# Half copies and a new product order in joined gate/up blocks, with sums between HBM tensors in longer rows

## Chip, core and metric

One core of one Trainium2 chip. The metric is the device time of the kernel in microseconds, the median of the runs of one comparison. Engines are named as in the profile: PE (TensorE, matmuls), PEld (its weight loads), DVE (VectorE), ACT (ScalarE), POOL (GpSimd), SP (the queue that issues the loads).

## What is computed

With S = 2048 rows, D = 512 and F = 1792, all in float32:

```python
g = sigmoid((x * gate_w).sum(-1))            # one gate per row
a = x @ dft_hid_re.T ; b = x @ dft_hid_im.T  # DFT over the 512 columns
A = dft_seq_re @ a - dft_seq_im @ b          # DFT over the 2048 rows, real part
B = (relu(x @ W_gate) * (x @ W_up)) @ W_down # gated ReLU unit
out = g * A + (1 - g) * B
```

## The kernel before

**Arithmetic.** Each operand is split into a high and a low part in fp32r, and a product is three matmuls (lo by hi, hi by lo, hi by hi; `PARTS`). Products of 2x2 block matrices are done by the seven-product scheme of Strassen and Winograd, `LEFT` and `RIGHT` being the sums that go into products 1 to 7. A product over one 512-column half is 6 matmuls of 128x128 by 128x512. There are 3423 matmuls.

**PSUM.** Its eight banks form four pairs x, m, y, t (`PAIRS`), one bank for each half i of a product. `BANK` says where a product accumulates: 1 and 2 in x, 5 and 3 in m, 6 and 7 in y, 4 in t. Product 1 is copied from x to y, and 6 and 7 go on accumulating there; the value of y after product 6 (`s6`) and that of m after product 5 (`s5`) are copied to SBUF. After product 7 ACT copies -y to t, on which product 4 accumulates, and DVE adds u22 = y + s5. After product 3 DVE adds u12 = m + s6.

**Stages in order.** The gate/up stage has 7 block columns c: two at the start (for q=0 alone), c=2 by `Block` for q=0 and q=1, then c=3 to 6, in each of which one `Joined` block for q=0 and one for q=1 share a product set with `JointW` (the left-out corner products of both q, 3 matmuls each, in bank pair x; their evacuations are jv and jo). `JointX` makes the x forms (jx) for them once. In `Joined` the q=0 block has product 1 in y rather than x. Then come four spectral blocks (the DFT over columns: spectral for q=0 twice, q=1 twice), two late gate/up blocks (`Block(1, ...)`), two Down stages, and the Sequence, Joint and Last stages (the DFT over rows). In the profile the c=2 blocks end at 82 us, the spectral blocks begin at 233, the late blocks take 311 to 349.

**Other streams around these.** Results of a gate/up block (h0, h1 and their sums hs) are stored to the HBM tensor hd by POOL. POOL also issues `joint_sums` (l.1052): 32 DMAs from HBM to HBM, half of them accumulating, that form sums of the DFT matrices in the tensor td, which the Joint stages read from 528 us on. Gates (`gate`) load x rows (gx) on SP, reduce on DVE and put sigmoids in gs; `gate_store` writes them to HBM. `h_late` reloads h of a block (hk) and makes the sums that were left out at the start. The matrix x21 of q=1 is loaded and split again ahead of the spectral stage, since its buffers were given up.

**What sets the order.** The program records steps with a key, the index of a matmul: `pe(n, ...)` adds n matmuls, `op(key, ...)` any other step. `Plan.due` works back from the matmuls when a step must be done, and `Plan.order` goes through all engines and picks steps by a table of costs written in the kernel. The steps are emitted in that order, so each engine runs its own list in order, and 51 SBUF buffers of 4 KB a partition are handed from step to step, the longest idle first. DMAs on SP and POOL are issued in order as well, each behind those ahead of it. Every instruction is recorded by line 126. Two engines that read one PSUM bank are put one behind the other.

Of the kernel before, what the change touches and what calls it, by code (L numbers as in the profile page):

```python
# [10 lines left out]
AF = mybir.ActivationFunctionType  # L11
# [4 lines left out]
N = 512  # L16
# [112 lines left out]
class Plan:  # L129
# [14 lines left out]
    def op(self, key, f, *a):  # L144
        self.ops.append((key, len(self.ops), f, a))

    def pe(self, n, f, *a):
        self.op(self.now, f, *a)
        self.now += n
# [129 lines left out]
def kernel(ctx: ExitStack, tc, xP, xG, wgu, wd, cr, ci, wri, gw, out):  # L279
# [24 lines left out]
    plan = Plan()  # L304
    op, pe = plan.op, plan.pe
# [7 lines left out]
    td = hbm("td", 2, 4, 2, P, 2, N)  # L313
# [31 lines left out]
    def E():  # L345
        return plan
# [4 lines left out]
    def f32(ap):  # L351
        return ap.bitcast(F32)

    def combine(o, a, b, sign):
        (plan.vector.tensor_add if sign > 0 else plan.vector.tensor_sub)(o, a, b)
# [4 lines left out]
    def store(o, i, **k):  # L360
        plan.gpsimd.dma_start(out=o, in_=i, **k)

    def accumulate(o, i, **k):
        plan.gpsimd.dma_start(out=o, in_=i, accum_op=OP.add, **k)
# [9 lines left out]
    def x_load(q, b, ks=slice(0, 2)):  # L374
        k, j, o = int(b[0]) - 1, int(b[1]) - 1, piece[q, b]
        return lambda: load(o[:, ks], xP[2 * q + j, k, :, ks])
# [132 lines left out]
    class Block:  # L509
# [31 lines left out]
        def evac(self, m, key):  # L541
            x, y, p, t = (self.banks[k] for k in "xymt")
            e = E()

            def rectified(r, j, ps, sign):
                g, h = self.g[r], self.h[int(r[0]) - 1][:, j]
                op(key, lambda: e.scalar.activation(g.all, ps[0], AF.Relu, scale=sign))
                if sign > 0:
                    op(key + 1, lambda: e.vector.tensor_mul(h, g.all, ps[1]))
                else:  # L550
                    op(key + 1, lambda: e.vector.scalar_tensor_tensor(h, ps[1], sign, g.all, op0=OP.mult, op1=OP.mult))

            def added(r, ps, s):
                self.added(r, ps, s, key)

            if m == 1:
                op(key, lambda: e.scalar.copy(y.all, x.all))
            elif m in (5, 6):
                op(key, lambda: e.scalar.copy(self.s[m].all, (p if m == 5 else y).all))
            elif m == 2:  # L560
                rectified("11", 0, x, 1.0)
            elif m == 7:
                op(key, lambda: e.scalar.activation(t.all, y.all, AF.Copy, scale=-1.0))
                added("22", y, self.s[5])
            elif m == 3:
                added("12", p, self.s[6])
            elif m == 4:
                rectified("21", 0, t, -1.0)
# [7 lines left out]
    class Joined(Block):  # L576
# [6 lines left out]
                self.s[1] = buf("s1")  # L583

        def run(self, joint=None):
            slots = {(1, 1): (5, 1), (6, 1): (6,), (3, 0): (3, 7), (3, 1): (2, 4)}
            for m, i in (*((m, i) for m in ((1, 5) if self.q else (5, 1)) for i in range(2)), (6, 0), (6, 1), (3, 0), (7, 0), (7, 1), (3, 1), (4, 0), (4, 1)):
                pe(6, self.product, m, i)
                if i:
                    self.evac(m, plan.now)  # L590
                for y in slots.get((m, i), ()) if joint else ():
                    joint.step(y)
# [5 lines left out]
        def one(self, m, i, k, n):  # L598
            w, x, ps = self.w.of(m, i, k), self.x[m], self.banks["y" if m == 1 and not self.q else BANK[m]]
            a, b = PARTS[n]  # L600
            mm(ps[i], w[a], x[b][:, k], start=m in FIRST and k == n == 0, stop=m in (3, 4) and k == 1 and n == 2)

        def evac(self, m, key):
            y, t = self.banks["y"], self.banks["t"]
            if m == 1 and not self.q:
                op(key, lambda: E().scalar.copy(self.s[1].all, y.all))
            elif m == 7:
                for i in range(2):
                    op(key, lambda i=i: E().scalar.activation(t[i], y[i], AF.Copy, scale=-1.0))
                self.added("22", y, self.s[5], key)  # L610
            else:
                super().evac(m, key)

    class JointX:


        def __init__(self, key):
            a, b = (piece[q, "21"] for q in range(2))
            raw = [buf(f"jx{n}") for n in range(2)]
            t5, t6, t7, t4 = raw[0][:, 0], raw[0][:, 1], raw[1][:, 0], raw[1][:, 1]  # L620
            self.x = {}
            for n, (y, src, f) in enumerate((
                    (1, a[:, 0], None), (5, t5, (b[:, 0], a[:, 0])), (6, t6, (b[:, 1], t5)), (3, b[:, 1], None),
                    (7, t7, (b[:, 1], b[:, 0])), (2, a[:, 1], None), (4, t4, (a[:, 1], t6)))):
                x = self.x[y] = buf(f"jx{y}", dtype=F32R)
                if f:
                    op(key + 16 * n, lambda src=src, f=f: combine(src, *f, -1))
                op(key + 16 * n + 4, lambda x=x, src=src: E().scalar.copy(x[:, 0], src))
                op(key + 16 * n + 8, lambda x=x, src=src: E().vector.tensor_sub(x[:, 1], src, f32(x[:, 0])))

    class JointW:

# [419 lines left out]
    def joint_sums(m, hh, key):  # L1052
        def c(b):
            return (cr, ci)[m][2 * int(b[1]) - 2, 1, 2 * int(b[0]) - 2 + hh]

        for n, (o, first, second) in enumerate(((0, "11", "12"), (1, "12", "22"), (2, 0, "22"), (3, 2, "21"))):
            op(key + 30 * n, lambda o=o, i=first: store(td[m, o, hh], c(i) if isinstance(i, str) else td[m, i, hh], max_dma_last_dim=2 * N))
            op(key + 30 * n + 15, lambda o=o, i=second: accumulate(td[m, o, hh], c(i), max_dma_last_dim=2 * N))

# [77 lines left out]
    w = ws[1]  # L1139

    for n in range(4):
        joint_sums(n // 2, n % 2, 300 + 150 * n)

    spectral = Spectral()

# [5 lines left out]
    for c in range(2, NP):  # L1151
        w = prepared(c)
        if c == 2:
            for b in ("22", "11", "12", "21"):
                x_piece(1, b)
                op(plan.now - 100, x_load(1, b))
            for n, m in enumerate(ORDER):
                x_prep(1, m, plan.now - 46 + 24 * n)
            jx = JointX(plan.now + 70)
            for q in range(2):  # L1160
                Block(q, w).run()
        else:
            pair = [Joined(q, w) for q in range(2)]
            joint = JointW(w, jx, plan.now)
            for q, b in enumerate(pair):
                b.run(None if q else joint)
                b.done(plan.now + 8, joint)
    for q in range(2):
        x_piece(q, "21")
        op(plan.now - 150 + 60 * q, x_load(q, "21"))  # L1170
        x_prep(q, 2, plan.now - 100 + 100 * q)

    for t in range(NT):
        gate(t, plan.now + 30 + 50 * t)
    op(plan.now + 300, gate_store)
    for n, b in enumerate(BLOCKS):
        op(plan.now - 84 + n, spectral.load, b)
# [8 lines left out]
        return Left(source)  # L1186

    for c in range(2):
        h_late(0, c, plan.now + 30 * c)
    lefts = [spectrum(f) for f in range(2)]  # L1190
    for ih in range(2):
        SpectralBlock(spectral, 1, ih)
# [5 lines left out]
    key = plan.now  # L1198
# [83 lines left out]
```

## Time and profile before

| | us |
|---|---|
| median of the runs (788.25, 789.84, 790.48) | 789.84 |
| profiled execution | 789.34 |
| its span | 787.6 |
| PE busy | 779.2 |
| DVE busy | 635.0 |
| ACT busy | 403.6 |
| POOL busy | 116.4 |

The prediction quotes rows of four views. The page has busy times and the chain that ended last. The timeline has one instruction in a row: start in us, duration in us (a PE duration is a modelled end, so matmuls overlap; look at starts), engine, line, operation, output<-inputs by buffer name without number, shape, and in brackets the idle time of the engine just before it with what ended that. The view of a tile tells who waited for it. A group row has the count, busy us and mean ns of one.

### The profile page before, as it was taken

The numbers are of one execution on the slowest core, as the hardware profiler recorded it, in microseconds if no ns is written. First come the engines' busy times: TensorE is split into PE (matmuls) and PEld (weight loads), VectorE is DVE, ScalarE is ACT, GpSimd is POOL, SyncE is SP. The second block draws the span as 40 slices with busy tenths as digits, with TensorE's granted clock in tenths as the row PEclk, the third lists the DMA queues.
The fourth block names the chain that finished last, engine by engine and source line by source line (L and its number), as shares of the span: only waits on it lengthen the run. The fifth ranks groups of instructions, "written<-read, shape, count | busy, mean of one in ns | idle before, by whom it ended". The sixth has DMA issues, their size and how long they took to land.

```text
span 787.6 us, 9450 instructions
## 1 busy us (share of the span) xinstructions
PE 779.2 (99%) x3423; PEld 641.2 (81%) x3423; DVE 635.0 (81%) x700; ACT 403.6 (51%) x465; POOL 116.4 (15%) x160
## 2 busy tenths in 40 slices
PE   9999999999999999999999999999999999999997
PEld 7888788888887888888888888888888888888885
DVE  6999886868689423988764899977999999989963
ACT  6665443434355334476545464544757365565540
POOL 0020342333212121110000000200020001000200
PEclk9999999999999999999999999999999999999999
DMA  8373799979976998488688789849999889599914
GB/s 324 126 263 101 212 286 232 258 196 270 308 228 239 347 419 304 134 270 292 187 270 319 272 299 322 196 151 288 378 328 285 246 262 187 166 326 373 249 33 81
DMA packets 64287, 197.52 MB, mean 251 GB/s; under 512 B 6768, under 2 KB 15216, under 8 KB 64240
## 3 DMA queue, kind: packets, MB, share of 16 engines
q1 hardware_dynamic: 36656, 119.31, 42.5%
q0 software_dynamic: 27584, 77.60, 37.7%
q8 instruction: 27, 0.44, 0.2%
q14 instruction: 20, 0.16, 0.1%
HBM read 135.53 MB, written 69.75 MB: 261 GB/s over the span
## 4 chain that ended last, share of the span: by engine, by line
PE 84%; DMA 6%; issue 5%; DVE 2%; POOL 2%; ACT 1%; SPq 0%; POOLq 0%; ACTq 0%; DVEq 0%
PE ps L126 84%; DMA td<-ci 3%; DMA hd<-hs 2%; DMA td<-td 2%; POOL td L126 1%; POOL hd L126 1%; DVE u L126 1%; DVE h L126 1%; DMA wr<-wgu 0%; DVE hs L126 0%; ACT jch L126 0%; DVE v L126 0%; DVE z L126 0%; DVE vl L126 0%; DVE xl L126 0%
## 5 line engine op out<-in xcount | busy, mean ns | idle before, releaser
L126 PE MATMUL ps<-ch,ll 128*128 128x512 f32 x580 | 225.6, 389 | 0.0
L126 PE MATMUL ps<-cl,lh 128*128 128x512 f32 x580 | 225.6, 389 | 0.0
L126 PE MATMUL ps<-ch,lh 128*128 128x512 f32 x580 | 225.6, 389 | 0.0
L126 ACT CAST ch<-r 128x1024 fp32r<-128x1024 f32 x96 | 97.2, 1051 | 63.2 <-DVE r L126 52.6
L126 PEld LDWEIGHTS ps<-cl,lh 128*128 128x128 f32 x580 | 108.9, 188 | 22.7
L126 PEld LDWEIGHTS ps<-ch,ll 128*128 128x128 f32 x580 | 108.9, 188 | 22.6
L126 PEld LDWEIGHTS ps<-ch,lh 128*128 128x128 f32 x580 | 108.9, 188 | 22.5
L126 DVE TENSOR_TENSOR cl<-r,ch 128x1024 fp32r<-128x1024 f32 x96 | 114.6, 1219 | 2.4 <-ACT ch L126 2.0
L126 ACT COPY s<-ps 128x1024 f32<-128x1024 f32 x48 | 48.8, 1016 | 65.6 <-PE ps L126 59.4
L126 ACT ACTIVATE ps<-ps 128x1024 f32<-128x1024 f32 (+1 forms) x42 | 33.8, 805 | 89.0 <-PE ps L126 59.5
L126 DVE TENSOR_TENSOR cl<-hr,ch 128x1024 fp32r<-128x1024 f32 (+1 forms) x56 | 59.5, 1087 | 18.4 <-ACT ch L126 16.5
L126 ACT CAST ch<-hr 128x1024 fp32r<-128x1024 f32 (+1 forms) x56 | 51.4, 944 | 27.3 <-PE ps L126 19.7
L126 POOL DMA_DIRECT2D out<-z x23 | 17.0, 739 | 316.2 <-DVE z L126 310.9
L126 DVE TENSOR_TENSOR r<-r,r 128x1024 f32<-128x1024 f32 x48 | 57.1, 1218 | 0.0
L126 PE MATMUL ps<-xh,wb0l 128*128 128x512 f32 x112 | 44.0, 393 | 0.5 <-DVE u L126 0.5
L126 PE MATMUL ps<-vh,xl 128*128 128x512 f32 x112 | 43.7, 390 | 0.7 <-ACT s L126 0.7
L126 PE MATMUL ps<-xh,wb1l 128*128 128x512 f32 x112 | 43.9, 392 | 0.1
L126 PE MATMUL ps<-vl,xh 128*128 128x512 f32 x112 | 43.7, 390 | 0.0
L126 PE MATMUL ps<-xl,wb0h 128*128 128x512 f32 x112 | 43.6, 389 | 0.0
L126 PE MATMUL ps<-xh,wb0h 128*128 128x512 f32 x112 | 43.6, 389 | 0.0
L126 PE MATMUL ps<-vh,xh 128*128 128x512 f32 x112 | 43.6, 389 | 0.0
L126 PE MATMUL ps<-xl,wb1h 128*128 128x512 f32 x112 | 43.6, 389 | 0.0
(152 smaller groups left out, 1334.3 us busy)
## 6 DMA issues: line engine op xcount, KB each, us to landing
hr<-hd SPq DMA_DIRECT2D x42, 512.0 KB, 4.5
r<-cr SPq DMA_DIRECT2D x32, 512.0 KB, 6.8
r<-ci SPq DMA_DIRECT2D x32, 512.0 KB, 8.2
hd<-hs POOLq DMA_DIRECT2D x28, 512.0 KB, 8.8
out<-z POOLq DMA_DIRECT2D x23, 512.0 KB, 6.6
ad<-a POOLq DMA_DIRECT2D x16, 512.0 KB, 8.4
l<-ad SPq DMA_DIRECT2D x16, 512.0 KB, 8.0
r<-r POOLq DMA_DIRECT2D x16, 512.0 KB, 7.8
```

Of the source, the lines that this page charges most:

```text
L126: getattr(getattr(nc, self.engine), self.name)(*map(ap, self.a), **{k: ap(x) for k, x in self.k.items()})
```

## The change

1. **Order in joined blocks** (`Joined.run`). Before, q=0 began with products 5, 1 and q=1 with 1, 5; then 6, (3, half 0), (7, half 0), (7, half 1), (3, half 1), 4. Now both have 1, 5, 6, (3, 0), (7, 0), (3, 1), (7, 1), 4. The joint products 5 and 1 come behind (5, 1).
2. **Halves** (`half`). The copy to s6 behind product 6 and the copy of -y to t behind product 7 are issued for each half as soon as it is done. u22 is added behind both.
3. **JointX** starts at matmul +50 rather than +70, at a spacing of 12 rather than 16.
4. **joint_sums**: rows of 4 KB (8N bytes) instead of 1 KB; one set's steps are 50 matmuls apart rather than 15; sets begin at 300+130n rather than 300+150n.
5. **Later**: the load of x21 of q=1 from -90 to +70 (relative to the spectral start), and its split from 0 to +120; gates from +30+50t to +70+60t; the late sums from +30c to +180+40c.

The matmuls are the same in number and kind.

```diff
@@ -583,9 +583,11 @@
                 self.s[1] = buf("s1")
 
         def run(self, joint=None):
-            slots = {(1, 1): (5, 1), (6, 1): (6,), (3, 0): (3, 7), (3, 1): (2, 4)}
-            for m, i in (*((m, i) for m in ((1, 5) if self.q else (5, 1)) for i in range(2)), (6, 0), (6, 1), (3, 0), (7, 0), (7, 1), (3, 1), (4, 0), (4, 1)):
+            slots = {(5, 1): (5, 1), (6, 1): (6,), (3, 0): (3, 7), (3, 1): (2, 4)}
+            for m, i in [(m, i) for m in (1, 5, 6) for i in range(2)] + [(3, 0), (7, 0), (3, 1), (7, 1), (4, 0), (4, 1)]:
                 pe(6, self.product, m, i)
+                if m in (6, 7):
+                    self.half(m, i, plan.now)
                 if i:
                     self.evac(m, plan.now)
                 for y in slots.get((m, i), ()) if joint else ():
@@ -600,15 +602,20 @@
             a, b = PARTS[n]
             mm(ps[i], w[a], x[b][:, k], start=m in FIRST and k == n == 0, stop=m in (3, 4) and k == 1 and n == 2)
 
+        def half(self, m, i, key):
+            y = self.banks["y"][i]
+            if m == 6:
+                op(key, lambda: E().scalar.copy(self.s[6][:, i], y))
+            else:
+                op(key, lambda: E().scalar.activation(self.banks["t"][i], y, AF.Copy, scale=-1.0))
+
         def evac(self, m, key):
-            y, t = self.banks["y"], self.banks["t"]
+            y = self.banks["y"]
             if m == 1 and not self.q:
                 op(key, lambda: E().scalar.copy(self.s[1].all, y.all))
             elif m == 7:
-                for i in range(2):
-                    op(key, lambda i=i: E().scalar.activation(t[i], y[i], AF.Copy, scale=-1.0))
                 self.added("22", y, self.s[5], key)
-            else:
+            elif m != 6:
                 super().evac(m, key)
 
     class JointX:
@@ -624,9 +631,9 @@
                     (7, t7, (b[:, 1], b[:, 0])), (2, a[:, 1], None), (4, t4, (a[:, 1], t6)))):
                 x = self.x[y] = buf(f"jx{y}", dtype=F32R)
                 if f:
-                    op(key + 16 * n, lambda src=src, f=f: combine(src, *f, -1))
-                op(key + 16 * n + 4, lambda x=x, src=src: E().scalar.copy(x[:, 0], src))
-                op(key + 16 * n + 8, lambda x=x, src=src: E().vector.tensor_sub(x[:, 1], src, f32(x[:, 0])))
+                    op(key + 12 * n, lambda src=src, f=f: combine(src, *f, -1))
+                op(key + 12 * n + 4, lambda x=x, src=src: E().scalar.copy(x[:, 0], src))
+                op(key + 12 * n + 8, lambda x=x, src=src: E().vector.tensor_sub(x[:, 1], src, f32(x[:, 0])))
 
     class JointW:
 
@@ -1054,8 +1061,8 @@
             return (cr, ci)[m][2 * int(b[1]) - 2, 1, 2 * int(b[0]) - 2 + hh]
 
         for n, (o, first, second) in enumerate(((0, "11", "12"), (1, "12", "22"), (2, 0, "22"), (3, 2, "21"))):
-            op(key + 30 * n, lambda o=o, i=first: store(td[m, o, hh], c(i) if isinstance(i, str) else td[m, i, hh], max_dma_last_dim=2 * N))
-            op(key + 30 * n + 15, lambda o=o, i=second: accumulate(td[m, o, hh], c(i), max_dma_last_dim=2 * N))
+            op(key + 100 * n, lambda o=o, i=first: store(td[m, o, hh], c(i) if isinstance(i, str) else td[m, i, hh], max_dma_last_dim=8 * N))
+            op(key + 100 * n + 50, lambda o=o, i=second: accumulate(td[m, o, hh], c(i), max_dma_last_dim=8 * N))
 
 
 
@@ -1139,7 +1146,7 @@
     w = ws[1]
 
     for n in range(4):
-        joint_sums(n // 2, n % 2, 300 + 150 * n)
+        joint_sums(n // 2, n % 2, 300 + 130 * n)
 
     spectral = Spectral()
 
@@ -1156,7 +1163,7 @@
                 op(plan.now - 100, x_load(1, b))
             for n, m in enumerate(ORDER):
                 x_prep(1, m, plan.now - 46 + 24 * n)
-            jx = JointX(plan.now + 70)
+            jx = JointX(plan.now + 50)
             for q in range(2):
                 Block(q, w).run()
         else:
@@ -1167,11 +1174,11 @@
                 b.done(plan.now + 8, joint)
     for q in range(2):
         x_piece(q, "21")
-        op(plan.now - 150 + 60 * q, x_load(q, "21"))
-        x_prep(q, 2, plan.now - 100 + 100 * q)
+        op(plan.now - 150 + 220 * q, x_load(q, "21"))
+        x_prep(q, 2, plan.now - 100 + 220 * q)
 
     for t in range(NT):
-        gate(t, plan.now + 30 + 50 * t)
+        gate(t, plan.now + 70 + 60 * t)
     op(plan.now + 300, gate_store)
     for n, b in enumerate(BLOCKS):
         op(plan.now - 84 + n, spectral.load, b)
@@ -1186,7 +1193,7 @@
         return Left(source)
 
     for c in range(2):
-        h_late(0, c, plan.now + 30 * c)
+        h_late(0, c, plan.now + 180 + 40 * c)
     lefts = [spectrum(f) for f in range(2)]
     for ih in range(2):
         SpectralBlock(spectral, 1, ih)

```

**Where it moves instructions.** First DVE's list at the change from c=2 to c=3, from the last steps of the q=1 block of c=2. u22 and u12 are that block's sums, ps is PSUM, ws, wal, wb0l and wb1l are weights of c=3, jws and jw the joint weights, jx the joint x forms, h the results. Before:

```order
L126 TENSOR_TENSOR wb0l_700<-ws0_677,wb0h_694 128x1024
L126 TENSOR_TENSOR jws_707<-wr0_626 128x128
L126 TENSOR_TENSOR u22_711<-ps_76,s5_648 128x1024
L126 TENSOR_TENSOR jws_707<-jws_707,wr0_626 128x128
L126 TENSOR_TENSOR jws_707<-wr0_626 128x128
L126 TENSOR_TENSOR jws_707<-wr0_626,jws_707 128x128
L126 TENSOR_TENSOR h0_725<-g11_681,ps_76 128x512
L126 TENSOR_TENSOR ws1_732<-wr0_626,wr1_641 128x512
L126 TENSOR_TENSOR jw_728<-jws_707,jw_728 128x512
L126 TENSOR_TENSOR u12_744<-ps_76,s6_665 128x1024
L126 TENSOR_TENSOR ws1_732<-wr0_626,ws0_677 128x512
```
After:

```order
L126 TENSOR_TENSOR ws0_679<-ws0_679,wr0_631 128x512
L126 TENSOR_TENSOR jx7_684<-jx1_663,jx7_684 128x512
L126 TENSOR_TENSOR jws_712<-wr0_631 128x128
L126 TENSOR_TENSOR jws_712<-jws_712,wr0_631 128x128
L126 TENSOR_TENSOR u22_717<-ps_76,s5_650 128x1024
L126 TENSOR_TENSOR wb0l_725<-ws0_679,wb0h_708 128x1024
L126 TENSOR_TENSOR jws_712<-wr0_631 128x128
L126 TENSOR_TENSOR jws_712<-wr0_631,jws_712 128x128
L126 TENSOR_TENSOR h0_736<-g11_691,ps_76 128x512
L126 TENSOR_TENSOR jx4_698<-jx1_663,jx4_698 128x512
L126 TENSOR_TENSOR u12_747<-ps_76,s6_667 128x1024
L126 TENSOR_TENSOR jw_739<-jws_712,jw_739 128x512
```
u22 now stands ahead of wb0l and has no wait on ACT any more; ACT's copy of -y waits for it instead. u12 follows the x form jx4 and comes ahead of jw and ws1.

Then ACT's list in the q=1 block of c=5 from the copy of product 1 to the halves of -y: s5 and s6 are the copies out of PSUM, the two ACTIVATE rows of 512 columns copy -y to t by halves, CAST rows split weights. Before:

```order
L126 COPY ps_76<-ps_76 128x1024
L126 COPY s5_1527<-ps_76 128x1024
L126 CAST wah_1539<-wr0_1490 128x1024
L126 CAST jw_1551<-jws_1525 128x512
L126 COPY s6_1556<-ps_76 128x1024
L126 CAST wb0h_1563<-ws0_1546 128x1024
L126 ACTIVATE ps_76<-ps_76 128x512 x2
```
After:

```order
L126 COPY ps_76<-ps_76 128x1024
L126 COPY s5_1528<-ps_76 128x1024
L126 CAST wah_1539<-wr0_1493 128x1024
L126 COPY s6_1548<-ps_76 128x512
L126 CAST jw_1555<-jws_1534 128x512
L126 COPY s6_1548<-ps_76 128x512
L126 CAST wb0h_1571<-ws0_1560 128x1024
L126 ACTIVATE ps_76<-ps_76 128x512 x2
```
s6 was one row of 1024 columns behind the jw cast; it is two of 512 now, and the first stands ahead of that cast.

Last POOL's list in c=6 and at the spectral start, with the td sums from HBM to HBM and the stores of h to hd. Before:

```order
L126 DMA hd_68<-hs0_1647 128x2x512
L126 DMA hd_68<-hs1_1656 128x2x512
L126 DMA td_70<-td_70 512x256
L126 DMA td_70<-ci 512x256
L126 DMA hd_68<-h0_1764 128x512
L126 DMA hd_68<-h1_1741 128x2x512
L126 DMA hd_68<-hs0_1789 128x2x512
L126 DMA hd_68<-hs1_1800 128x2x512
L126 DMA hd_68<-h1_1914 128x2x512
L126 DMA hd_68<-h0_1919 128x512
```
After:

```order
L126 DMA hd_68<-hs0_1651 128x2x512
L126 DMA td_70<-td_70 128x1024
L126 DMA hd_68<-hs1_1660 128x2x512
L126 DMA td_70<-td_70 128x1024
L126 DMA td_70<-ci 128x1024
L126 DMA hd_68<-h0_1747 128x512
L126 DMA hd_68<-h1_1778 128x2x512
L126 DMA td_70<-ci 128x1024
L126 DMA hd_68<-hs0_1791 128x2x512
L126 DMA hd_68<-hs1_1800 128x2x512
L126 DMA td_70<-td_70 128x1024
L126 DMA hd_68<-h1_1942 128x2x512
```
The td rows stood as a pair ahead of a block's four stores, each waiting for the one before; now single ones stand between the stores, in rows of 1024 elements, and the last of them come later.

## The prediction, made before the changed kernel ran

> **What bounds the kernel now.** I read the page first (busy shares, chain), then the timeline around every place where TensorE starts a matmul late.
>
> ```profile
> span 787.6 us, 9450 instructions
> PE 779.2 (99%) x3423; PEld 641.2 (81%) x3423; DVE 635.0 (81%) x700; ACT 403.6 (51%) x465; POOL 116.4 (15%) x160
> PE 84%; DMA 6%; issue 5%; DVE 2%; POOL 2%; ACT 1%; SPq 0%; POOLq 0%; ACTq 0%; DVEq 0%
> ```
> TensorE is busy 99% of the span and leads the chain. The change leaves all 3423 matmuls in, so the time can fall only by gaps between them. The spacing without a gap:
>
> ```profile
> 329.87 0.39 PE L126 MATMUL ps<-xh,wal 128*128 128x512 f32 x1
> 332.59 0.39 PE L126 MATMUL ps<-xh,wb0l 128*128 128x512 f32 x1
> ```
> These start two consecutive products of 12 matmuls: 2.72 us, 0.227 us each. Whatever a start lies behind its predecessor beyond 0.227 us is loss. Such starts behind the first 26 us are few; I take each loss from the starts, since the wait in brackets counts only the part in which nothing ran.
>
> First place, the end of the c=2 blocks:
>
> ```profile
> 81.57 1.22 DVE L126 TENSOR_TENSOR u<-ps,s 128x1024 f32<-128x1024 f32 x1
> ...
> 82.00 0.39 PE L126 MATMUL ps<-xh,wd 128*128 128x512 f32 x1
> 82.84 0.50 PE L126 MATMUL ps<-xh,wb0l 128*128 128x512 f32 x1 [0.46 <-DVE u L126]
> 83.18 0.40 PE L126 MATMUL ps<-xl,wb0h 128*128 128x512 f32 x1
> ```
> Product 5 of c=3 overwrites bank pair m while DVE still adds u12 out of it. Loss (82.84-82.00-0.23)+(83.18-82.84-0.23) = 0.73 us; the second part shows that the matmul behind a stall comes 0.11 us late too. Second place, a q=1 block of c=5:
>
> ```profile
> 187.88 1.01 ACT L126 COPY s<-ps 128x1024 f32<-128x1024 f32 x1 [0.56 <-ACT jw L126]
> ...
> 188.50 0.39 PE L126 MATMUL ps<-xh,wb1h 128*128 128x512 f32 x1
> ...
> 188.95 0.50 PE L126 MATMUL ps<-xh,wb1l 128*128 128x512 f32 x1
> ...
> 189.29 0.39 PE L126 MATMUL ps<-xl,wb1h 128*128 128x512 f32 x1
> ```
> Product 7 accumulates on bank pair y, so it waits for the s6 copy, which sat behind a cast of jw: 0.34 us. Third place, the first spectral block:
>
> ```profile
> 242.73 1.22 DVE L126 TENSOR_TENSOR xl<-x,xh 128x1024 fp32r<-128x1024 f32 x1
> ...
> 244.06 0.39 PE L126 MATMUL ps<-vh,xh 128*128 128x512 f32 x1
> 244.06 1.01 ACT L126 COPY s<-ps 128x1024 f32<-128x1024 f32 x1 [3.98 <-DVE xl L126]
> ...
> 245.12 0.50 PE L126 MATMUL ps<-vh,xl 128*128 128x512 f32 x1 [0.68 <-ACT s L126]
> ...
> 245.46 0.39 PE L126 MATMUL ps<-vl,xh 128*128 128x512 f32 x1
> ```
> The s6 copy waited 3.98 us for DVE's xl, the last reader of the buffer that s6 takes over: 0.83+0.11 = 0.95 us. Behind it, at 248.33 and 248.66, vl came late for another 0.12+0.11 = 0.23:
>
> ```profile
> 247.98 0.39 PE L126 MATMUL ps<-vh,xl 128*128 128x512 f32 x1
> 248.19 1.22 DVE L126 TENSOR_TENSOR vl<-v,vh 128x1024 fp32r<-128x1024 f32 x1
> ...
> 248.33 0.50 PE L126 MATMUL ps<-vl,xh 128*128 128x512 f32 x1
> ```
> Why was DVE so late? Because of POOL, which issues in order:
>
> ```profile
> 219.37 1.08 POOL L126 DMA_DIRECT2D td<-ci  x1 [7.83 <-DMA td<-td]
> 220.04 1.71 POOL L126 DMA_DIRECT2D hd<-h  x2
> ...
> 232.89 2.35 DVE L126 TENSOR_TENSOR u<-ps,s 128x1024 f32<-128x1024 f32 x2 [2.43 <-DMA hd<-h]
> ...
> 234.12 1.05 ACT L126 CAST vh<-v 128x1024 fp32r<-128x1024 f32 x1 [2.44 <-DMA hd<-hs]
> ```
> A td sum waited 7.83 us for the td sum ahead; the h stores queued behind it landed late, and u12, u22 and vh needed their buffers.
>
> The other excess starts lie ahead of 26 us or in the Joint stages, in rows that the change leaves alone. All that this change can remove is 0.73+0.34+0.95+0.23 = **2.25 us**.
>
> **The change part by part.**
>
> *Products 1, 5 in that order for q=0.* Product 1 of a q=0 block goes to bank pair y, product 5 to m. At the c=2/c=3 boundary product 5 moves 12 matmuls, 2.72 us, later; u12 was only 0.6 us late. The 0.73 goes. What is late next is y: u22 and the copy of -y must leave it, long before.
>
> *New order on DVE there.* The order puts u22 of the last c=2 block ahead of ACT's copy of -y from the same banks; it was behind.
>
> ```profile
> 70.98 0.69 DVE L126 TENSOR_TENSOR jx<-x,jx 128x512 fp32r<-128x512 f32 x1
> 71.59 0.69 DVE L126 TENSOR_TENSOR jx<-x 128x512 f32<-128x512 f32 x1
> ...
> 76.98 1.01 ACT L126 ACTIVATE ps<-ps 128x1024 f32<-128x1024 f32 x1 [1.47 <-PE ps L126]
> ...
> 78.02 1.23 DVE L126 TENSOR_TENSOR u<-ps,s 128x1024 f32<-128x1024 f32 x1 [1.05 <-ACT ps L126]
> ...
> 79.50 0.39 PE L126 MATMUL ps<-xh,wd 128*128 128x512 f32 x1
> ```
> From the jx row at 70.98 DVE now has that one and seven more of 512 columns (the joint x forms among them, which come earlier now) (0.60 us apart, 70.98 to 71.59), wal (1.13) and two short jws (about 0.2 each): 70.98+4.8+1.13+0.4 = 77.3. u22 ends at 78.55, ACT's copy at 79.6 to 79.7, and product 4, which accumulates on t, wanted 79.50. I take **+0.30** (0.2 and the 0.11 behind it); bounds 0 (DVE 0.3 us earlier) and 0.6 (0.3 later).
>
> *Products 6 and 7 by halves.*
>
> ```profile
> L126 ACT ACTIVATE ps<-ps 128x512 f32<-128x512 f32 x16 | 9.3, 582 | 25.3 <-PE ps L126 15.8 <-DVE u L126 9.4
> ```
> A half takes 0.58 us where the whole took 1.01. The first half of s6 is copied during the second half of product 6, the second has six matmuls of product 3 and six of 7 ahead of its need, 12 x 0.227 = 2.7 us, where the whole copy had 1.36. The jw cast no longer comes first. The 0.34 goes, at no price on ACT (two starts more per block, on an engine 51% busy). The new tight place is product (4,1) on the second half of t: (7,1) ends, ACT is done 0.16+0.02+0.58 = 0.78 us later, (4,1) starts 6 x 0.227 = 1.36 us later: 0.55 to spare, if ACT is free. u22 follows ACT on DVE (0.78+1.23 = 2.0 us after (7,1)) and the next block's product in y comes at 2.72: 0.7 to spare. Cost nothing; bounds 0 and, if a cast of 1.05 us stood in the way at one of eight blocks, 0.6.
>
> The row charges ACT's halves with 9.4 us behind DVE's u, so two readers of one bank stand in line here. The Trainium skill's page "PSUM — Partial Sum Buffer", section "PSUM bank collisions raise a hardware error", asks for that: accesses of two engines to one bank and quadrant must be kept apart, reads too. It speaks against halves mixed with u22; if reads could overlap, the 0.30 above would be 0. Who goes first is the next rival's question.
>
> *td sums in 4 KB rows, 50 matmuls apart (11.3 us).*
>
> ```profile
>   POOL td L126: 67.2, 15
> DMA to landing us min/median/max: 3.2/8.1/11.7
> r<-r POOLq DMA_DIRECT2D x16, 512.0 KB, 7.8
> ```
> POOL stood 67.2 us before td. Sums now follow at 11.3 us, over the median landing 8.1 and near the worst 11.7, which was among 1 KB rows; r<-r, accumulates whose 512 KB go as 128 rows of 4 KB, land in 7.8 (median). So h stores no longer queue, and by the stalls' rows u12 and u22 come 2.4 us and vh 2.4 us sooner. The remade x21 of q=1 moves 120 matmuls, 27 us, later, so s6 takes another buffer. Then s6 is copied at its product's end, and 0.95+0.23 go. Bounds: 0 to 1.18 gained.
>
> *Gates and late sums later.* Gate loads have 8 us to spare. Eight late sums move into a stretch where DVE is full:
>
> ```profile
> 310.00:320.00 10.00, 10.00 (x46) 8.29 (x45) 9.96 (x12) 5.70 (x6) 1.43 (x2) 1.00 0.51 189
> 328.44 1.22 DVE L126 TENSOR_TENSOR u<-ps,s 128x1024 f32<-128x1024 f32 x1
> L126 DVE TENSOR_TENSOR hs<-hs,h 128x512 f32<-128x512 f32 x18 | 12.4, 688 | 0.3
> ```
> u12 at 328.44 ended 2.9 us before product 5 of the next block (332.59). The eight sums (0.6 us apart, 4.9 us) come ahead of it, and the lr3, wb1l, one ws1 and one h (4.3 us) fall behind it: u12 keeps about 2.4 us. What falls behind has idle DVE time after 336 to be made up. Price 0; bounds 0 and 3.5 (the slower rival).
>
> **Sum.** -0.73-0.34-0.95-0.23+0.30 = -1.95 against the profiled execution's 789.34: 787.4. The median of the runs before, 789.84, lies 0.50 above that execution; I carry this over: **787.9**.
>
> **Rivals.** (a) *All goes, nothing new:* DVE reaches u22 by 77.0, no 0.30: 787.6. For it: 0.3 us of DVE is easily won. Against it: no u22 has been that early.
> (b) *Part of it stays or comes back:* td sums among the block's loads still land after 11.3 us, POOL holds the h stores and the spectral stall stays (1.18), or the 79.50 wait is 0.6 and one half copy meets a cast: 787.9+0.6 to 1.2 = 788.5 to 789.1. For it: the worst landing, 11.7. This includes that the new spacing does not do what it says.
> (c) *Late sums block DVE (slower):* the loads of their inputs (hk) now stand on SP behind the gate stores:
>
> ```profile
> 290.62 13.54 SPq L126 DMA_DIRECT2D gd<-gx  x8
> DMA to landing us min/median/max: 3.1/7.0/8.2
> 310.02 1.22 DVE L126 TENSOR_TENSOR a<-ps,s 128x1024 f32<-128x1024 f32 x1
> ```
> Eight gate stores held SP 13.54 us; hk landed in 3.1 to 8.2 us. The stores ended at 304.2; three loads (0.4 each) and the first hk come behind, so the hk are issued by about 306, and at 8.2 us land by 314. DVE reaches the sums at 316.4: after the a12 sum below (308.0 on the new clock, 2 us sooner) come 8.4 us of its own, ws and l sums. Only beyond 316.4+2.4 = 319 does product 5 wait. If the stores start 6 us later and hk takes 12 us, DVE stands until about 322.5: 3.5 us, 791.4.
> (d) *DVE first at every joined block:* if u22 read y ahead of ACT's second half, the half would end 0.2+1.23+0.6 = 2.05 us after (7,1), 0.7 late for (4,1), 0.8 with the matmul behind: eight blocks, 6.5 us, 794.4. The order has ACT first there, and u22 waits for it. This is where the page's rule would decide.
>
> **Chances.** Forecast 0.54 (787.2 to 788.5), (a) 0.16 (787.0 to 787.9), (b) 0.18, (c) 0.09, (d) 0.03. The range 786.8 to 790.2 holds the first three but for a tenth (the runs before spread 2.2 us), and leaves (c) and (d) out. 0.3%, about what a measurement of this kernel can tell from no change, is 2.4 us: faster is below 787.47, which takes a quarter of the forecast and over half of (a) with some runs' luck, 0.25; slower is above 792.2, part of (c) and (d), 0.08; the same 0.67.
>
> **What would show it.** Right: no excess start at 82 to 84, 188 to 190 and 243 to 249; one of about 0.2 us near 79.5; POOL's wait for td near 0; spectral s6 copy released by PE. Wrong: PE waits on ACT ps in the joined blocks (halves), on DVE u near 328 (late sums), or on s again at the spectral start.

## The result and the profile after

The changed kernel takes 786.48 us (median of 9 runs, 786.20 to 786.89), the kernel before 788.68 (9 runs beside them, 788.05 to 792.81). The ratio over all these runs is 0.996 (95% interval 0.9944 to 0.9976); it is the ratio of the means, 786.51 and 789.68, and that of the medians would be 0.9972, since the kernel before has some long runs. The forecast was 787.9 in a range of 786.8 to 790.2: right in direction, but the gain was larger, and the time lies 0.3 us below the range.

The page of the changed kernel, its profiled execution being one of 786.80 us; the chain that ended last is 99% PE now:

```profile
span 785.0 us, 9454 instructions
PE 778.5 (99%) x3423; PEld 643.1 (82%) x3423; DVE 634.1 (81%) x700; ACT 404.4 (52%) x473; POOL 111.9 (14%) x160
PE 99%; DVE 0%; ACT 0%; issue 0%; ACTq 0%; DVEq 0%
```

PE's waits in the changed kernel, all of them. The column after the colon is the sum in us, then the count and the longest:

```profile
PE ps L126 <- DVE warm L126: 1.2, 1, 1.2
```

The one at the very start is all that PE itself shows; waits of its weight loads (PEld) have rows of their own, and two of those remain in the Joint stages (e14 below). To see where the time came from I take, for each stage, the distance between the first matmul of the stage and that of the next, less 0.2267 us for each matmul between them. The first real matmul is the one behind 15 on the tile warm. The excess in us:

| stage (matmuls) | before | changed |
|---|---|---|
| first real matmul starts at | 5.17 | 4.77 |
| first two blocks (168) | 0.89 | 1.62 |
| c=2 (168) | 0.62 | 0.05 |
| c=3 to 6 (660) | 0.96 | 0.00 |
| spectral blocks (336) | 1.27 | 0.01 |
| late blocks, Down (756) | 0.03 | 0.00 |
| the rest, Joint stages in it | 0.73 | 0.75 |

The three middle rows lost 2.85 and keep 0.06; the start took 0.33 more in this execution (4.77+1.62 against 5.17+0.89), and the end behind the last matmul is 0.1 shorter. That makes 785.0 against 787.6.

The change from c=2 to c=3 in the timeline of the changed kernel:

```profile
77.42 1.22 DVE L126 TENSOR_TENSOR u<-ps,s 128x1024 f32<-128x1024 f32 x1
78.67 1.01 ACT L126 ACTIVATE ps<-ps 128x1024 f32<-128x1024 f32 x1 [1.22 <-DVE u L126]
79.60 0.39 PE L126 MATMUL ps<-xh,wb1h 128*128 128x512 f32 x1
79.83 0.41 PE L126 MATMUL ps<-xh,wd 128*128 128x512 f32 x1
80.07 0.39 PE L126 MATMUL ps<-xl,wd 128*128 128x512 f32 x1
...
82.37 0.39 PE L126 MATMUL ps<-xh,wd 128*128 128x512 f32 x1
82.60 0.39 PE L126 MATMUL ps<-xh,wal 128*128 128x512 f32 x1
```

DVE reaches u22 at 77.42 (77.3 was forecast), and ACT's copy ends at 79.68. PE starts product 4 at 79.83, without a gap of more than 0.02: the stall of 0.30 that the forecast paid for did not come. That is not owed to PE's start, which was 0.3 us later in this execution. In e4, e6, e12 and e14 below, which have the same order here, product 4 starts between 79.34 and 79.66, and u22 starts 2.40 to 2.41 us ahead of it in all five: DVE moves along with PE. The forecast had 79.50-77.3 = 2.2 us between the two. Product 1 follows at 82.60 without a gap.

ACT's copies of s6 by halves in the q=1 block of c=5, where 0.34 was lost:

```profile
185.97 0.59 ACT L126 COPY s<-ps 128x512 f32<-128x512 f32 x1
186.45 0.63 ACT L126 CAST jw<-jws 128x512 fp32r<-128x512 f32 x1
186.97 0.60 ACT L126 COPY s<-ps 128x512 f32<-128x512 f32 x1
```

The first half is away before the jw cast. At the spectral start s6 waits for nothing that belongs to x21:

```profile
240.60 1.02 ACT L126 COPY s<-ps 128x1024 f32<-128x1024 f32 x1 [1.59 <-issue]
```

And the sums between HBM tensors, from the view of td and that of DMAs (KB each and the median from issue to landing in us at the end):

```profile
  POOL td L126: 44.7, 7
td<-cr POOLq DMA_DIRECT2D x12, 512.0 KB, 8.2
td<-ci POOLq DMA_DIRECT2D x12, 512.0 KB, 9.7
td<-td POOLq DMA_DIRECT2D x8, 512.0 KB, 9.1
```

POOL still waited 44.7 us for td (67.2 before). Rows of 4 KB do not land sooner than those of 1 KB, whose medians in the kernel before were 7.2, 9.5 and 7.2 us. Over all 32 sums, the view of td between 40 and 300 us has 8.1 (median) and 11.7 (worst) before, 9.0 and 14.0 now. This part of the forecast did not come true, though the stall that it was to remove is gone. So the question for the experiments was which part removed what.

### The profile page after: what moved, and what is told of

It reads as the page before. It is cut to its first block, busy times and chain, and to the rows that moved or that the text cites. A ratio compares the mean times of both kernels' runs of the same rounds, so it can differ in the third digit from the quotient of the medians.

```text
span 785.0 us, 9454 instructions
## 1 busy us (share of the span) xinstructions
PE 778.5 (99%) x3423; PEld 643.1 (82%) x3423; DVE 634.1 (81%) x700; ACT 404.4 (52%) x473; POOL 111.9 (14%) x160
## 3 DMA queue, kind: packets, MB, share of 16 engines
q0 software_dynamic: 21440, 77.60, 36.9%
## 4 chain that ended last, share of the span: by engine, by line
PE 99%; DVE 0%; ACT 0%; issue 0%; ACTq 0%; DVEq 0%
PE ps L126 99%; ACT jch L126 0%; DVE v L126 0%; DVE z L126 0%; ACT js L126 0%; DVE warm L126 0%; ACTq L126 0%; DVEq L126 0%
## 5 line engine op out<-in xcount | busy, mean ns | idle before, releaser
L126 ACT COPY s<-ps 128x1024 f32<-128x1024 f32 (+1 forms) x56 | 50.1, 894 | 56.7 <-PE ps L126 55.1
```

The source lines that it names most:

```text
L126: getattr(getattr(nc, self.engine), self.name)(*map(ap, self.a), **{k: ap(x) for k, x in self.k.items()})
```

## Experiments

Four theories were at stake. **Places**: each part takes the stalls at its own places. **Transfers**: the lighter HBM traffic does all. For the spectral start, **POOL** (the prediction's): h stores queued behind td make u, vh and vl late; and **buffer**: s6 waits because it takes over x21's buffer. A profile is of one execution; medians and ranges are of 4 to 12 runs, beside 18 to 35 of the kernel before on the same chip. The ratios are the record's, over all these runs, and not ratios of the medians.

| run | median us (range) | ratio to before (interval) |
|---|---|---|
| e1 sums only | 788.82 (788.28 to 792.18) | 0.9996 (0.9983 to 1.0008) |
| e2 order only | 787.88 (786.78 to 791.85) | 0.9974 (0.9957 to 0.9990) |
| e3 x21 only | 788.41 (788.04 to 788.87) | 0.9986 (0.9973 to 0.9998) |
| e9 gates, late sums only | 788.26 (788.09 to 788.89) | 0.9985 (0.9975 to 0.9996) |
| e10 order and x21 | 786.84 (786.44 to 787.32) | 0.9969 (0.9958 to 0.9979) |
| e4 changed, old sums | 786.79 (786.45 to 788.75) | 0.9965 (0.9955 to 0.9975) |
| e5 changed, old order | 787.86 (787.59 to 789.97) | 0.9980 (0.9969 to 0.9992) |
| e6 changed, x21 early | 786.57 (786.42 to 786.77) | 0.9963 (0.9949 to 0.9976) |
| e13 changed, old order, halves | 787.15 (786.88 to 787.54) | 0.9969 (0.9957 to 0.9981) |
| e12 changed, whole copies | 798.48 (798.23 to 798.96) | 1.0111 (1.0093 to 1.0129) |
| e14 changed, js first | 785.78 (785.63 to 786.11) | 0.9950 (0.9937 to 0.9963) |
| e11 before, other buffer | 789.99 (787.97 to 795.31; one more of 868.29 left out) | 1.0009 (0.9992 to 1.0027) |
| e15 before, no store buffers | 788.89 (788.14 to 790.08) | 0.9988 (0.9976 to 1.0000) |
| e16 x21 only, store buffers | 789.04 (788.18 to 792.97) | 0.9995 (0.9982 to 1.0009) |
| e17, e18, one run each | 791.09, 792.60 | |

The medians of the kernel before in these comparisons were 789.30, 788.87, 789.82 and 789.81, with runs from 787.9 to 793.0; one more, of 1321.71, is left out.

**e1 and e2: one half of the change each, from the kernel before.** e1 has only the sums part of the diff:

```diff
-            op(key + 30 * n, ... max_dma_last_dim=2 * N))
+            op(key + 100 * n, ... max_dma_last_dim=8 * N))
-        joint_sums(n // 2, n % 2, 300 + 150 * n)
+        joint_sums(n // 2, n % 2, 300 + 130 * n)
```

> The kernel before with part 4 of the change alone (sums between HBM tensors in 4 KB rows, 50 matmuls apart). Theory of places: time is the floor of back-to-back matmuls plus the stalls at single places, and this part takes only those at the spectral start (0.95 and 0.23 us), because the stores of h are no longer queued behind sums on POOL. Then 1.2 us under the kernel before; the stalls near 83 (0.73) and in a q=1 block (0.34) stay; the spread of the runs, if it comes from the landing of 1 KB rows, falls from 4.8 us to under 1. Rival (transfers alone): the joined blocks' order does nothing and the lighter HBM traffic brings it all: 2.2 us or more under, no stall left.

Measured: no gain that can be told from nothing, where places expected 1.2 us, and the runs still reach 792. Its profiled execution keeps the stall near 83; near 189 only 0.07 is left of 0.34, though the row of c=3 to 6 still loses 0.88 (0.96 before). At the spectral start 0.54 is left of 1.27, which one execution can't tell from chance (e17 below). s6 waits for the same reason as before, with POOL's wait for td down to 39.4 us:

```profile
243.49 1.02 ACT L126 COPY s<-ps 128x1024 f32<-128x1024 f32 x1 [3.33 <-DVE xl L126]
```

That speaks against transfers, against the POOL theory as the whole cause, and against the part of places that expected the spectral start to be cleared by the sums. e2 has only class `Joined` of the changed kernel (order, halves).

> The kernel before with parts 1 and 2 alone (order of products in joined blocks, halves). Theory of places: takes 0.73 near 83 and 0.34 near 189 and the short ones of under 0.1 in other joined blocks, 1.1 to 1.4 us under the kernel before; the stall at the spectral start stays (about 1.2), and so does the wide spread of the runs. Rival (transfers alone): no different from before.

Measured: 787.88; excess in the c=2 and c=3 to 6 rows 0.00 and 0.12 (before 0.62 and 0.96), and 1.33 at the spectral start. For the joined blocks places holds: the order and the halves take 1.46 and leave the spectral start alone. The best run, 786.78, is at the changed kernel's time, the others up to 791.85.

**e4 and e5: one half undone, from the changed kernel.** e4 turns the sums back, e5 class `Joined`.

> The changed kernel with part 4 undone (1 KB rows, old spacing and starts). Theory of places: stalls at the spectral start come back as far as late stores of h make them, but x21 and the gates stay later, so 0.2 to 1.2 us over the changed kernel, and POOL waits for td some 60 us. Rival (transfers alone): 2 us over, the time of the kernel before.

Measured: 786.79, 0.3 over the changed kernel, no stall between 30 and 550 us, and this with td as much in POOL's way as ever (one of its runs took 788.75):

```profile
  POOL td L126: 65.7, 15
td<-ci POOLq DMA_DIRECT2D x12, 512.0 KB, 8.4
td<-td POOLq DMA_DIRECT2D x8, 512.0 KB, 7.2
```

So the sums part is not needed; whether it brings the 0.3, which lies between runs of two comparisons, stays open. The prediction's cause, "So h stores no longer queue", is not what removed the stall here.

> The changed kernel with parts 1 and 2 undone (old order, whole copy of s6). Theory of places: stalls of about 0.7 near 83 and 0.3 in q=1 blocks come back, 1.0 to 1.4 us over the changed kernel, no stall at the spectral start. Rival (transfers alone): the changed kernel's time.

Measured: 787.86, 1.4 over the changed kernel, with excess of 0.34 and 0.95 in the two rows of the joined blocks, and 0.03 at the spectral start. Places again, but near 83 only 0.45 of the 0.73 came back (0.34 in the row of c=2 and 0.11 behind it). The rest must have gone with JointX's earlier start, by elimination: it is the one other part that moves steps there, and e1, e3 and e9, which have the remaining parts one by one, keep 0.61 to 0.62 in that row. It had no run of its own.

**e3, e6, e9, e10: which part clears the spectral start.** e3 moves only x21 (its two lines of the diff), e6 moves it back in the changed kernel, e9 moves only the gates and late sums, e10 is e2 with e3.

> The kernel before with only the load and split of x21 of q=1 moved later (from part 5). Buffer theory: the stall at the spectral start comes from the buffer that s6 takes over from x21, and moving x21 is enough without any change to the sums between HBM tensors: 1.0 to 1.3 us under the kernel before, stalls near 83 and 189 stay, POOL still waits about 65 us for td, and the wide spread of the runs narrows. POOL theory (the prediction's): stores of h are still late behind td, so vl and u come late and half of the stall or more stays; 0.2 to 0.6 us under before.

> The changed kernel with x21 of q=1 loaded and split early again. Buffer theory: s6 waits for DVE's xl again, a stall of 0.3 to 1.2 us near 243, that much over the changed kernel, though POOL hardly waits for td. POOL theory: h stores are in time, so xl is too, and the time is the changed kernel's within 0.2.

> The kernel before with only the gates and the late sums moved later (the rest of part 5). Both theories: DVE's xl still stands ahead of the gates in its list, so the stall at the spectral start stays; within 0.4 us of the kernel before. A third theory, that the gates' work on DVE and their loads make the spectral start late, would take 1.0 us or more. If the late sums cost anything at the late blocks, a gap shows near 330.

> The kernel before with parts 1 and 2 (order, halves) and the later x21, nothing else: sums in 1 KB rows, JointX, gates and late sums as before. Buffer theory: no stall is left between 30 and 550 us, so this is the changed kernel's time, 2.2 to 2.8 under before, within 0.3 of the changed kernel. POOL theory: a stall of 0.5 us or more stays at the spectral start.

Measured: e3 clears the spectral start (excess 0.03) and its runs lie within 0.9 us. But e6 does not bring the stall back, and e9 clears it too (0.01), which neither the buffer nor the POOL theory had foreseen. A third theory had, that the gates' work on DVE makes the spectral start late; but e3 clears the stall with the gates where they were, so their move is not needed for it. e10 is the changed kernel within 0.4. What is common? In e9 and e6 the split of x21 is as late on DVE as before, but s6 does not wait for it, the same row in e9 being

```profile
241.83 1.01 ACT L126 COPY s<-ps 128x1024 f32<-128x1024 f32 x1 [0.81 <-PE ps L126]
```

The emitted program tells why: any of these edits makes the planner hand out the buffers otherwise. Only in the kernel before, e1 and e2 does s6 take over x21's. That put the blame not on the lateness of x21 but on who inherits its buffer.

**e11: the buffer alone.** All engines' lists as in the kernel before; s6 may not take over x21's buffer. The line that decides (`names` holds the last owner of each buffer):

```diff
-                u = min(range(UNITS), key=lambda u: (held[u] >= n, idle[u]))
+                u = min(range(UNITS), key=lambda u: (held[u] >= n, b.name == "s6" and names[u] == "x121", idle[u]))
```

> The kernel before with every engine's list of instructions as it was, and one buffer handed out otherwise: s6 may not take over x21's, so s6 of the first spectral block follows h0 and the next weight part follows x21. Buffer theory: the 0.95 us near 245 go though POOL waits for td as long as before and the h stores are as late; the 0.23 behind it may stay; 0.5 to 1.2 us under the kernel before at the median, and the wide spread of its runs (788 to 793) narrows. POOL theory: the late stores hold u and vl, so a stall of 0.5 us or more stays near 245, and the spread stays too.

Measured: its profiled execution, 787.97, has no stall at the spectral start (0.05), but the others reach 795 and the median is that of the kernel before. The theory that this one buffer is the whole cause fell.

**e15 to e18: buffers with a store on them.** In the kernel before and e11, vh2 and vl2 (the split weights of the second spectral product) take over the buffers of hs0 and hs1, and u12 that of h1, all of which POOL stores to hd; in e11 s6 took over that of h0, stored too. In e3 and e9, vh2 and vl2 follow vs5 and a weight; in the changed kernel vh2, vl2 and s6 follow a weight, vs5 and v21, none of them a stored result. e17 and e18 run the kernel before and e11 once more for another profile.

> The kernel before once more, for a profile of another execution. Store-buffer theory: whatever its time is above 788.0 shows as excess starts of matmuls between 233 and 262 us, behind waits on stores of h; the stalls near 83 and 189 are the same as ever. Rival: the excess is spread over the span, or in other stages.

> The kernel before with another buffer for s6 once more, for a profile of another execution; its runs spread from 788 to 795. Store-buffer theory: in an execution over 788.5 PE waits between 233 and 262 us for vl, vh or u, not for s6, and ACT or DVE waited on stores of h. Rival: elsewhere.

Measured: 791.09 and 792.60, both slower than the profiled execution of the prediction, and both slow at the place named: excess at the spectral start 2.30 and 4.23, 0.62 in c=2 as ever. In e17 the joined blocks ahead lost 1.51 in place of 0.96, which the expectation had not foreseen: at 227.19 PE waits for an s6 copy of c=6, 0.59 lost. DVE and ACT had come late there behind the first wait below, of ACT's g for a store. Waits of the kernel before in e17, between 215 and 262 us:

```profile
ACT g L126 <- DMA hd<-hs: 3.0, 1, 3.0
ACT vh L126 <- DMA hd<-hs: 2.6, 1, 2.6
DVE u L126 <- DMA hd<-h: 1.8, 1, 1.8
```

And the timeline of e18, s6 on the buffer of h0:

```profile
244.34 0.39 PE L126 MATMUL ps<-vh,xh 128*128 128x512 f32 x1
245.98 1.01 ACT L126 COPY s<-ps 128x1024 f32<-128x1024 f32 x1 [5.62 <-DMA hd<-h]
247.04 0.50 PE L126 MATMUL ps<-vh,xl 128*128 128x512 f32 x1 [2.32 <-ACT s L126]
...
248.26 0.63 PE L126 MATMUL ps<-vl,xh 128*128 128x512 f32 x1
248.68 0.63 PE L126 MATMUL ps<-vh,xh 128*128 128x512 f32 x1
249.11 0.63 PE L126 MATMUL ps<-vh,xl 128*128 128x512 f32 x1
```

I had moved s6 from one bad buffer to a worse one: a store that had not landed. PE waited for s6 again, where the expectation had named vl, vh or u; it lost 2.5 us there, and then some more (below). e15 is the kernel before with seven of these buffers (vh2, vl2, vl4, s6, xh2, u12, u22) taken from elsewhere, all lists as they were; e16 is e3 with vh2 and vl2 put on hs0 and hs1. The edits are conditions in the line shown for e11, for example in e16:

```diff
+                u = min(range(UNITS), key=lambda u: (held[u] >= n, 960 < s.key < 1060 and (names[u] in ("hs0", "hs1")) != (b.name in ("vh2", "vl2")), idle[u]))
```

> The kernel before with every engine's list as it was; only the buffers of the spectral start are handed out otherwise: vh2, vl2, vl4, s6, xh2, u12 and u22 take none whose last user is a store of h or x21's split. Store-buffer theory: no stall at the spectral start in any run, POOL waits for td as before, runs within about 1 us of each other, median about 788.3, as with x21 moved. Rival (transfers themselves or the work on DVE are late, whoever holds the buffers): wide spread as before, median 789 to 790.

> The kernel with only x21 moved later (narrow runs, 788.0 to 788.9), lists as they were, but vh2 and vl2 made to take over the buffers of the two last stored sums hs. Store-buffer theory: waits of 1 to 3 us of ACT vh and DVE vl on the stores come back, runs spread over 1.5 us or more and the median rises by 0.3 to 1.5. Rival: no change from that kernel.

Measured: e16 brought the stall back (excess 1.03 against 0.03 in e3; the runs reach 792.97, the median rose by 0.6), with the wait named:

```profile
234.01 1.05 ACT L126 CAST vh<-v 128x1024 fp32r<-128x1024 f32 x1 [2.54 <-DMA hd<-hs]
...
239.70 0.50 PE L126 MATMUL ps<-vh,xl 128*128 128x512 f32 x1 [0.66 <-ACT ps L126]
```

e15 has no stall in its profiled execution and no run above 790.08 where the kernel before beside it reached 792.89, but its runs spread over 1.9 us where 1 was expected, and its gain of 0.12% just reaches no difference. Its h1 and h0 still took the buffers of hs0 and hs1, and the g of c=6 that of an earlier hs1, the one that e17 waited for. So buffers with stores on them are shown to make the stall (e16, e18). What counts is that the store lands late: in e6 vh2 follows an h1, which is stored too, and nothing waits. That such buffers are all of the spread is not shown: what e15's slower runs lose stays open.

**e12 and e13: order and halves apart.** e12 keeps the new order and copies s6 and -y whole, e13 the old order with halves.

> The changed kernel with the new product order, but s6 and -y copied whole (part 2 undone). Order theory: the order alone gives the copies room; s6 has 6 matmuls of product 3 as before, so the 0.34 near 189 and the short stalls of 0.07 in other q=1 blocks come back, and whole -y copies, needed six matmuls sooner relative to (7,1), cost 0.1 to 0.3 in up to eight blocks (copy done 0.16+0.02+1.01 = 1.2 us after (7,1), wanted at 1.36): 0.5 to 1.5 us over the changed kernel. Rival (halves do nothing): the changed kernel's time.

> The changed kernel with halves but the old product order. The halves take the stall of s6 (0.34 near 189 and the short ones), the order takes the one near 83: then 0.3 to 0.8 us over the changed kernel, with one stall at the change from c=2 to c=3. If order mattered in the q=1 blocks too: 1.2 over.

Measured: e12 is 12 us slower than the changed kernel. PE's waits in it:

```profile
PE ps L126 <- ACT ps L126: 9.2, 8, 1.3
```

In the new order (4, 0) follows directly on (7, 1). A whole copy of -y can begin only behind (7, 1), and both halves of product 4 want it at once: eight blocks lose 1.26 to 1.49, and 0.11 behind each. My expectation, 0.5 to 1.5 us in all, gave it six matmuls' room, which only the second half has. The first half of t has to be copied during (3, 1), as the changed kernel does it. e12 is coarser than the kernel before in one point: there -y went in two instructions, both behind (7, 1), here in one. Two would have the first half done 0.43 us sooner by the rows of both sizes (1.01 and 0.58), an estimate that no run checks. e13 is 0.67 over the changed kernel: with the halves alone the two rows of c=2 and c=3 to 6 lose 0.34 and 0.28 (0.34 and 0.95 in e5 without either), so the halves take the stalls of the q=1 blocks, and the order takes what is left of the one near 83.

**e14: the last two stalls.** The changed kernel still loses 0.34 at each of two places in the Joint stages, where a copy out of PSUM (js) stands behind casts on ACT. The first of them:

```profile
548.96 3.91 ACT L126 CAST jch<-jc 128x1024 fp32r<-128x1024 f32 x4
...
552.76 0.58 ACT L126 COPY js<-ps 128x512 f32<-128x512 f32 x1
552.94 0.39 PE L126 MATMUL ps<-jch,jlh 128*128 128x512 f32 x1
...
553.40 0.19 PEld L126 LDWEIGHTS ps<-jch,jll 128*128 128x128 f32 x1 [0.49 <-ACT js L126]
553.40 0.50 PE L126 MATMUL ps<-jch,jll 128*128 128x512 f32 x1
```

The planner gets a rule:

```diff
+            if s.writes and s.writes[0].base.name == "js":
+                s.due -= 2.0
-                    if found is None or t < found[0] - 0.12:
+                    if found is None or t < found[0] - (0.9 if found[1].writes and found[1].writes[0].base.name == "js" else 0.12):
```

> The changed kernel with one rule more in its planner: in the Joint stages the copy of a product's sum out of PSUM (js) goes ahead of a cast on ACT if it would start within 0.9 us. The two stalls that are left between 30 and 779 us, 0.34 each near 553 and 703, go: 0.5 to 0.7 us under the changed kernel, about 785.9. Rival (the cast moved behind is late in turn): PE waits on jch or jcl instead, no gain.

Measured: 785.78 (785.63 to 786.11), below every run of the changed kernel (786.20 and up, in another comparison). ACT takes the copy between two casts:

```profile
549.50 2.00 ACT L126 CAST jch<-jc 128x1024 fp32r<-128x1024 f32 x2
...
551.38 0.59 ACT L126 COPY js<-ps 128x512 f32<-128x512 f32 x1
...
551.86 1.06 ACT L126 CAST jch<-jc 128x1024 fp32r<-128x1024 f32 x1
```

Both gaps are gone: the excess of the last stages fell from 0.75 to 0.00. This is the fastest version run here.

## Why the prediction was wrong

**Bound and floor: right.** PE's back-to-back spacing carries the span, and the time fell by the gaps and nothing else.

**Products 1, 5: right.** 0.73 forecast; the c=2 row lost 0.57, and the 0.11 behind it went too. e2 shows it for order and halves together (0.62 to 0.00), e13 for the order (0.34 without it).

**Halves: right, and more.** 0.34 forecast; the c=3 to 6 row lost 0.96. That row also holds 0.11 of the stall near 83; of the other 0.51, 0.22 sat in three gaps of 0.07 at the same place of the other q=1 blocks, 0.08 in the q=0 blocks, the rest in delays of under 0.02. I had counted only starts over 0.3 us apart. So "All that this change can remove is 0.73+0.34+0.95+0.23 = 2.25 us" was too small: the three rows lost 2.85, of which these are 0.51 and the spectral row 0.09. Cost of the halves: none, as forecast.

**+0.30 at u22: order right, stall wrong.** u22 does go ahead of ACT's copy and ACT waits for it, but u22 starts 2.4 us ahead of product 4 where the sum had 2.2, and in none of the five profiles with this order does the c=2 row lose more than 0.05. Rival (a) had this; in e4, whose PE starts product 4 at 79.34, sooner than the 79.50 of the forecast, DVE reached u22 at 76.9.

**td sums: wrong.** "Sums now follow at 11.3 us ... So h stores no longer queue" did not happen: POOL still waits 44.7 us, since the landings did not shorten. e4 shows that the part is worth 0.3 us at most. The stall went since the buffers were handed out anew; e16 shows this for vh2 and vl2, for s6 it is argued from the emitted programs and the waits. The chain was read rightly up to a point (late h stores, then u and vh, then s6); which link the change cut was not.

**"The median of the runs before, 789.84, lies 0.50 above that execution; I carry this over": the step whose premise failed.** It took the scatter of the kernel before for a constant of the machine. Much of the scatter is stalls that the change removes. The two profiled executions of the kernel before, 789.34 and 791.09 (e17), differ by 1.75 us; 1.03 of that is the spectral start (1.27 and 2.30) and 0.55 the joined blocks. The best runs (787.9) are where e3 and e9 are (788.0 to 788.9), with no stall at the spectral start. The changed kernel has no such 0.5: its profiled execution, 786.80, is among its slowest runs. The nine runs of the kernel before beside it have a median of 788.68, below the profiled 789.34.

So 787.9 was 1.4 us too high by three terms: 0.50 carried over, 0.30 for a stall that did not come, and 0.60 of gaps not counted. Without the first two the same sum gives 789.34-2.25 = 787.1, and with all that the three rows of the table lost, 789.34-2.85 = 786.5. That the gain between the medians, 2.20 us, is near the 1.95 of the forecast is luck: the profiled executions are 2.54 apart, and the median before came out lower.

The bounds "0 to 1.18 gained" for the td part fell with it, as the stall changes from execution to execution (1.27 and 2.30 in the two profiled ones) and I had one sample. The rivals (c) and (d) did not occur: no wait stands near 330, and ACT goes ahead of u22 in the joined blocks. The premise of (b) came true (the worst landing of a td sum was 14.0 us, over the spacing of 11.3), its stall did not come. What (d) priced at 6.5 us is close in kind to e12, where both halves of t are late.

## What to carry to other kernels

When runs of a kernel spread by more than its gaps explain, profile further executions before pricing a stall: the stall behind DMA landings here differed from one execution to the next, and removing it removed much of the scatter of the baseline too. In a pool of recycled buffers, look up whose buffer a late step inherits; here a buffer that was still being stored tied ACT and DVE to POOL's queue, with which they had no other business. Order and granularity can hang together: the product order here is worth 0.7 us with half copies and costs 12 us with whole ones.

## What the runs showed of the hardware

In one execution a short pause of PE cost twice. In e18 PE stood 2.32 us, and from the fourth matmul behind it the starts were 0.427 us apart in place of 0.227, for eight matmuls: 1.6 us more. The view of windows, whose columns are the busy time of PE, then PEclk, DMA share and GB/s, has the granted clock at half for that time:

```profile
244.60:247.00 2.40, 0.12 (x1) 1.00 0.98 396
247.80:251.20 3.40, 3.40 (x9) 0.51 0.45 124
251.30:253.00 1.70, 1.70 (x9) 1.00 0.83 328
```

Pauses of 1.1 to 1.3 us (eight in e12) and 0.95 us (e17) had no such sequel. That the pause set off the half clock is read from this one sequence. The Trainium skill, page "TensorE: Matmul & The Clock Gate", section "What's actually happening", has the clock go to half after an idle window of about 3.4 us that runs freely, and back to full after a busy one of as long. The half speed and its duration of 3.4 us agree; the pause ahead of it was shorter here, 2.32 us.

Rows of 4 KB in place of 1 KB cut the packets of the software queue from 27584 to 21440, and the landing of a 512 KB sum between HBM tensors did not get shorter (medians 7.2 to 9.5 us with 1 KB, 8.2 to 9.7 with 4 KB, the sums being spaced otherwise too).
